# Attention transposes split into row halves over two pairs of PSUM banks, loads gated by GpSimd writes, and a longer count for one list's gathers

## The chip, the cores and the metric

The kernel runs on one core of one Trainium2 chip. The metric is the device time of one execution in microseconds (us), median of three runs. Engines are named as the profile names them: PE is the matrix engine, PEld its weight loads, DVE the vector engine, ACT the scalar engine, POOL is GpSimd, SP the engine that issues most transfers. "L416" is line 416 of the kernel.

## The reference

Windowed attention over 8 batches, 8 heads, 576 positions, head dimension 64, followed by a mixture of 8 experts with a fixed capacity. Cut to what is computed:

```
scores = q @ k^T / sqrt(D)                 # heads 0-3: 0 <= i-j < 32
                                           # heads 4-7: 0 <= i-j < 128 and (i-j) % 4 == 0
attn   = softmax(masked scores)
x      = (attn @ v) as [4608 tokens, 512]
logits = x @ w_gate                        # 8 experts
for idx in argsort(-logits.flatten()):     # best pair of token and expert first
    assign token to expert if the token is free and the expert holds < 576
out[tokens of e] = relu(x @ w1[e]) @ w2[e]
```

## The kernel before, in words

The program has two stages that follow each other. **Attention** works on 32 units, four for each batch: heads of kind 0 (plain window) or kind 1 (every fourth key), two units of two heads for each kind. A unit's 576 queries are nine blocks of 64 queries against 96 keys, two heads side by side in the 128 rows. It goes through the engines like this: PE makes the scores into two banks `pm` (L398); DVE masks them and keeps each row's extreme (L403) in `sc`; POOL subtracts that extreme (L409); PE transposes the nine blocks of `sc`, three into a bank of `pS` at a time (`turn`, L416); ACT takes the exponential out of `pS` into `et` (L412); PE multiplies with the values in two groups of five and four blocks into a bank of `px` (`values`, L424); ACT copies the sums (L428) and DVE divides (L433, L434) into `xs`. After the second unit of a kind, SP stores `xs` to the scratch tensor `xd`, and PE transposes `xs`, again three blocks into a bank, this time of `px` (`banks`, L475); ACT copies that to `xt`, from which the router's logits are made once per batch (L516, L548; L540 for the last). For each group of 128 tokens, DVE then makes 256 flags of "value reaches this step" (`coarse`, L647, into a ring of five tiles `pre`), and PE counts them per expert (L652) into a bank `pz` that keeps the sums until the end of the stage.

PSUM has eight banks: two `pm`, two `pS`, three `px`, one `pz`. The tiles for q, k and v are double-buffered by batch; a batch's twelve loads (eight of q and k, four of values) are issued on SP in a fixed order, each as soon as its tile is free of the batch two before.

**The experts' stage** makes eight lists of tokens one after the other, numbered r = 0 to 7 (the seventh list is r = 6). For a list it searches a threshold by counting (PE L660, DVE), turns the accepted tokens into row numbers (PE L1003, 18 small products, here called the placing), POOL gathers the rows of `xd` with five indirect transfers into `xg` (L1199), and PE transposes these by halves of 64 rows (`turn_halves`, L1254, 36 products). Then follow the two matrix products, `ph` (L1285) and `py` (L1327, L1330, L1332).

The order of instructions on each engine is fixed when the kernel is built. A planner (`Schedule`) takes operations with an engine, an estimated cost in ns, what they depend on and a `boost`; it computes a due time for each and places the earliest possible one by one. `lat` is an extra delay that it counts between an operation and its users; PSUM banks and their holders are part of the plan (`Pool`, `Buf`). The operation's `form` says in which shape of the array PE works; a change of form is counted at `T_TURN`. The chip runs every engine's list in that order, waiting on semaphores. The estimates set only the order.

Of the kernel before, what the change touches and what calls it, by code (L numbers as in the profile page):

```python
# [22 lines left out]
NE, FF = 8, 1024  # L23
# [19 lines left out]
ADDED, T_A, T_G = (("2", 0), ("1", 1), ("2", 1)), 2000, 4500  # L43
# [201 lines left out]
def attention(tc, ctx, C, load_const, T, xd, Lt, R):  # L245
# [24 lines left out]
    PM, PS, PV = Pool([banks_("pm", 2)]), Pool(banks_("pS", 2)), Pool(banks_("px", 3))  # L270
# [22 lines left out]
    ready = {}  # L293

    def load(b, kind, part):
# [5 lines left out]
        for t, src in ((QT, T["in_qd" if kind else "in_qp"]), (KT, T["in_kd" if kind else "in_kp"])):  # L301
            assert tuple(src.shape[1:]) == tuple(t[0][0].shape)
            ls.append(sp(1, lambda t=t, src=src: nc.sync.dma_start(t[kind][s][:, part], src[b][:, part]), load.old,
                            128 * 4 * S, b))
        ready["q", kind, b, part] = ls

    def load_values(b, kind):
# [4 lines left out]
        x = [sp(1, lambda c0=c0, c1=c1: nc.sync.dma_start(  # L312
            v[:, s, c0:c1], src[b].rearrange("p (c x) -> p c x", c=NV)[:, c0:c1]), before, 128 * (c1 - c0) * 4 * 65 * 4, b)
             for c0, c1 in ((0, 3), (3, NV))]
# [10 lines left out]
    class Unit:  # L325
# [17 lines left out]
        def build(self):  # L343
# [8 lines left out]
            for g, (c0, c1) in enumerate(GR):  # L352
# [6 lines left out]
                ex.append(e)  # L359
            olde = old("e", u % N_E)  # L360
            et = []
            for j in range(3):
                pt = Buf(PS)
                t = self.op("PE", 330, lambda j=j, pt=pt: self.turn(j, pt.tile, sc), [*ex[:1 + (j > 0)], ready["c", 1]], B_T, pt)
                uses.append(t)
                k = self.op("ACT", 400, lambda j=j, pt=pt: self.exps(j, pt.tile),
                            [t, *olde], B_T)
                pt.users.append(k)
                et.append(k)
# [44 lines left out]
        def turn(self, j, pt, sc):  # L414
            for x in range(3):
                nc.tensor.transpose(pt[:KB, 128 * x:128 * x + 128], sc[:, ORD[3 * j + x]], C["identf"])  # L416
# [39 lines left out]
    def banks(un, xs, done, usex):  # L456
# [8 lines left out]
        for i in range(3):  # L465
            pt = Buf(PV)

            def turn(i=i, pt=pt):
                t = pt.tile[:, :384]
                if kind:  # L470
                    t = t.rearrange("p (a c i) -> p a c i", a=2, c=3)
                else:
                    t = t.rearrange("p (a r c j) -> p a c r j", a=2, c=3, r=DIL)
                for c in range(3):
                    nc.tensor.transpose(t[:, :, c], xs[:, 3 * i + c].rearrange("p a d -> p (a d)"), C["identf"])  # L475
# [3 lines left out]
            def keep(i=i, pt=pt, f=nc.vector.tensor_copy if eng == "DVE" else act):  # L479
                t = pt.tile[:, :384].rearrange("p (a n) -> p a n", a=2)  # L480
                if kind:
                    f(xt[:, :, 192 * i:192 * i + 192], t)
                else:
                    x = xt.rearrange("p a (r n) -> p a r n", r=DIL)
                    f(x[:, :, :, 48 * i:48 * i + 48], t.rearrange("p a (r n) -> p a r n", r=DIL))

            t = un.op("PE", 330, turn, [*done, *oldt], late, pt)
            usex.append(t)
            k = un.op(eng, 450 + 100 * (eng == "DVE"), keep, [t, *oldt], late)
# [981 lines left out]
```

## Time and profile before

| | us |
|---|---|
| median of three runs | 653.42 (651.93 to 654.25) |
| profiled execution, its own time | 654.11 |
| span from first to last instruction | 652.3 |
| PE busy over the span | 615.5 (94%) |
| DVE busy | 451.9 (69%) |
| ACT busy | 305.8 (47%) |
| POOL busy | 196.8 (30%) |
| transfers | 100.18 MB, mean 154 GB/s |

Attention takes about the first quarter of the span, the experts the rest; between them lies a stretch in which the router works alone. A busy share is an average over stages with different limits, and PE's ends are modelled, so a price for a product is better read from the distance between two starts than from a duration. The profiled execution lies 0.7 us above the median.

### The profile page before, as it was taken

The page shows a single profiled execution, that of the slowest core. Times are in us where ns is not written, and L with a number is a line of the kernel's source. Part 1 is how long each engine was busy: PE and PEld are TensorE (multiplying, and loading weights), DVE is VectorE, ACT ScalarE, POOL GpSimd, SP SyncE. Part 2 cuts the span into 40 slices and gives each one's busy share as a digit, 9 for nine tenths or more (in the row PEclk, how much of TensorE's full clock was granted, in tenths as well). Part 3 has the DMA queues.
Part 4 walks back from the last instruction along what each step waited for, and adds up shares of the span by engine and source line. Part 5 has one row for each costly group of instructions (what it writes and reads, how often), then busy time and mean ns, then how long its engine had stood idle before and what let it go on. Part 6 is the DMA issues. An engine that isn't in the chain of part 4 may idle for free.

```text
span 652.3 us, 17966 instructions
## 1 busy us (share of the span) xinstructions
PE 615.5 (94%) x6748; PEld 530.0 (81%) x6749; DVE 451.9 (69%) x1930; ACT 305.8 (47%) x691; POOL 196.8 (30%) x326
## 2 busy tenths in 40 slices
PE   7999999997569999999999999999999989999994
PEld 5787888785449978977998898799889769989983
DVE  4668678885787888885997898699689746415200
ACT  3868788753038346844343433435244335325210
POOL 3434434330053156543016104301610530521011
PEclk9999999998579999999999999999999989999998
DMA  8998999823059378991164236207313734211010
GB/s 313 388 268 271 310 288 300 236 56 71 3 160 246 59 182 281 215 301 50 41 201 144 62 89 226 73 19 235 112 57 129 228 126 149 74 48 59 1 41 32
DMA packets 62680, 100.18 MB, mean 154 GB/s; under 512 B 7280, under 2 KB 26224, under 8 KB 62592
## 3 DMA queue, kind: packets, MB, share of 16 engines
q1 hardware_dynamic: 53216, 73.82, 35.6%
q0 software_dynamic: 9376, 25.21, 14.5%
q8 instruction: 53, 0.87, 0.5%
q14 instruction: 35, 0.29, 0.1%
HBM read 73.83 MB, written 18.87 MB: 142 GB/s over the span
## 4 chain that ended last, share of the span: by engine, by line
PE 70%; issue 12%; DVE 7%; DMA 4%; POOL 3%; ACT 2%; SPq 1%; POOLq 0%; DVEq 0%; ACTq 0%
PE ph L1285 25%; PE py L1327 18%; PE px L424 5%; PE pS L416 4%; PE pm L398 4%; PE pz L660 2%; PE px L475 2%; PE py L1330 2%; PE py L1332 2%; DVE sc L403 1%; POOL out L1353 1%; DMA xg<-xd,idx 1%; PE px L516 1%; DMA raw<-in_moe_w 1%; POOL xg L1199 1%
## 5 line engine op out<-in xcount | busy, mean ns | idle before, releaser
L1327 PE MATMUL py<-w2h,hb 128*128 128x512 f32 x512 | 165.9, 396 | 0.0
L1285 PE MATMUL ph<-xh,w1h 128*128 128x256 f32 (+1 forms) x512 | 138.6, 301 | 0.0
L1285 PE MATMUL ph<-xh,w1l 128*128 128x256 f32 (+1 forms) x512 | 136.3, 297 | 0.0
L1285 PE MATMUL ph<-xl,w1h 128*128 128x256 f32 (+1 forms) x512 | 135.9, 296 | 0.0
L1327 PEld LDWEIGHTS py<-w2h,hb 128*128 128x128 f32 x512 | 96.9, 189 | 20.0
L1071 ACT ACTIVATE hb<-ph 128x256 fp32r<-128x256 f32 (+2 forms) x192 | 59.9, 347 | 106.8 <-PE ph L1285 101.9
L1327 PE MATMUL py<-w2l,hb 128*128 128x512 f32 x256 | 100.4, 392 | 0.0
L1285 PEld LDWEIGHTS ph<-xh,w1h 128*128 128x128 f32 x512 | 91.4, 189 | 0.6 <-issue 0.3
L1285 PEld LDWEIGHTS ph<-xl,w1h 128*128 128x128 f32 x512 | 91.5, 189 | 0.1
L1285 PEld LDWEIGHTS ph<-xh,w1l 128*128 128x128 f32 x512 | 91.5, 190 | 0.0
L1353 POOL DMA_INDIRECT out<-y,tok x40 | 39.9, 998 | 148.6 <-ACT y L1071 68.7
L409 POOL TENSOR_TENSOR sc<-sc,mx 128x480 f32<-128x480 f32 x64 | 57.0, 912 | 90.2 <-DVE mx L403 90.2
L1071 ACT ACTIVATE y<-py 128x512 f32<-128x512 f32 (+1 forms) x40 | 23.9, 598 | 128.2 <-PE py L1327 97.9
L1305 DVE SCALAR_TENSOR_TENSOR hb<-ph,hb 128x320 fp32r<-128x320 f32 (+1 forms) x128 | 57.4, 453 | 32.6 <-ACT hb L1071 31.6
L403 DVE CUSTOM_DVE_ANT_0 sc<-pm,const 128x96 f32<-128x96 f32 x288 | 53.8, 253 | 21.8 <-PE pm L398 19.4
L1199 POOL DMA_INDIRECT xg<-xd,idx x40 | 43.6, 1089 | 64.7 <-issue 41.2
L1327 PEld LDWEIGHTS py<-w2l,hb 128*128 128x128 f32 x256 | 48.5, 189 | 9.3
L412 ACT ACTIVATE et<-pS 96x384 f32<-96x384 f32 x96 | 43.2, 484 | 23.8 <-PE pS L416 23.1
L1072 DVE TENSOR_TENSOR w2l<-raw,w2h 128x512 fp32r<-128x512 f32 x48 | 31.5, 684 | 20.2 <-ACT w2h L1071 19.9
L416 PE MATMUL pS<-const,sc 128*96 128x128 f32 x288 | 43.6, 279 | 1.0 <-ACT et L412 0.9
L1071 ACT ACTIVATE w1h<-raw 128x512 fp32r<-128x512 f32 x64 | 37.6, 628 | 6.2 <-DMA raw<-in_moe_w 6.1
L398 PE MATMUL pm<-k,q 64*64 64x96 f32 x1152 | 35.5, 253 | 2.7 <-DMA k<-in_kp 1.5
(188 smaller groups left out, 982.2 us busy)
## 6 DMA issues: line engine op xcount, KB each, us to landing
raw<-in_moe_w SPq DMA_DIRECT2D x128, 256.0 KB, 4.5
k<-in_kp SPq DMA_DIRECT2D x16, 304.0 KB, 6.0
k<-in_kd SPq DMA_DIRECT2D x16, 304.0 KB, 6.3
q<-in_qp SPq DMA_DIRECT2D x16, 288.0 KB, 5.4
q<-in_qd SPq DMA_DIRECT2D x16, 288.0 KB, 6.4
xd<-xs SPq DMA_DIRECT2D x64, 72.0 KB, 3.2
xd<-xs SPq DMA_DIRECT2D x16, 288.0 KB, 5.3
w2l<-raw POOLq DMA_DIRECT2D x16, 256.0 KB, 4.7
```

What stands on the lines that cost most here:

```text
L398: nc.tensor.matmul(o[w:w + 64], self.Q[c][r:r + 64], self.K[c][r:r + 64], start=True, stop=True)
L403: nc.vector.tensor_tensor_reduce(out=sc[:, c], in0=pms[g][:, c // 2 * KB:c // 2 * KB + KB], in1=mm[:, c if self.kind else min(1, c)], scal ...
L409: nc.gpsimd.tensor_tensor(sc[:, g::2], sc[:, g::2], mx[:, g::2, None].to_broadcast([128, n, KB]), op=OP.subtract)
L412: nc.scalar.activation(self.E0[:, 384 * j:384 * j + 384], pt[:KB, :384], AF.Exp, scale=-1.0)
L416: nc.tensor.transpose(pt[:KB, 128 * x:128 * x + 128], sc[:, ORD[3 * j + x]], C["identf"])
L424: nc.tensor.matmul(px[64 * a:64 * a + 64, x - c0], self.E0[:, w:w + 64], self.V[c][a], start=True, stop=True)
L1071: act = lambda o, i, f=AF.Copy: nc.scalar.activation(o, i, f)
L1199: nc.gpsimd.indirect_dma_start(out=xg[:n], out_offset=None, in_=xd, in_offset=bass.IndirectOffsetOnAxis(ap=box[0][:n, m:m + 1], axis=0))
L1285: nc.tensor.matmul(o, a[:, d * 128:d * 128 + 128], b[:, d, c0:c1], start=((d, i) == pairs[0]), stop=((d, i) == pairs[-1]))
L1305: hl = op("DVE", 335 if j == 0 else 400, lambda: nc.vector.scalar_tensor_tensor(hb[:, CAP + c0:CAP + c1], o, 0.0, hb[:, c0:c1], op0=OP.max ...
L1327: nc.tensor.matmul(py, x, w, start=(f + i == 0), stop=(f == NF - 1 and i == 2))
L1353: s = nc.gpsimd.indirect_dma_start(out=out, out_offset=bass.IndirectOffsetOnAxis(ap=box[1][:n, m:m + 1], axis=0), in_=y[:n], in_offset=None)
```

## The change

- `rows` (new) transposes a block as two halves of 64 rows, each into its own bank. `turn` and the transposes of `xs` use it, in groups of five and four blocks instead of three times three. `pS` becomes two tiles of two banks each and takes the transposes of `xs` too. ACT's exponential and copy take a group of five or four blocks out of two banks at once. `values` depends on its own group's exponential only.
- `px` shrinks from three banks to two, and the standing bank `pz` is gone from attention. The counts of flags go into a bank of `px`, for a whole batch in one operation (token group by token group for the last batch), and DVE adds them to a tile `cc` (`coarse_sum`). `pz` is made in the experts' stage, and cleared there by ACT.
- The loads of batch b+1 are planned during batch b. Ahead of each of the twelve, POOL writes one element of the tile to be loaded (`paced`), after one of batch b's eight subtractions; the load waits for that write.
- `T_GL`: the planner counts 7500 ns instead of 4500 after the gathers of list r = 6.

```diff
-ADDED, T_A, T_G = (("2", 0), ("1", 1), ("2", 1)), 2000, 4500
+ADDED, T_A, T_G, T_GL = (("2", 0), ("1", 1), ("2", 1)), 2000, 4500, 7500
...
-    PM, PS, PV = Pool([banks_("pm", 2)]), Pool(banks_("pS", 2)), Pool(banks_("px", 3))
+    PM, PV = Pool([banks_("pm", 2)]), Pool(banks_("px", 2))
+    PS = Pool([ps.tile([128, 2, 512], F32, name=f"pS{i}") for i in range(2)])
+
+    def rows(out, in_):
+
+        for h in range(2):
+            p = slice(64 * h, 64 * h + 64)
+            nc.tensor.transpose(out[:, h], in_[p], C["identf"][p, p])
...
+    def paced(after, to, deps):
+
+        un, e = after.pop(0)
+        return un.op("POOL", 100, lambda: nc.gpsimd.memset(to[:1, :1], 0.0), [e, *deps], B_A)
+
+    def load(b, kind, part, after=None):
...
+            deps = load.old
+            if after:
+                deps = [paced(after, to, deps)]
...
-            for j in range(3):
-                pt = Buf(PS)
-                t = self.op("PE", 330, lambda j=j, pt=pt: self.turn(j, pt.tile, sc), [*ex[:1 + (j > 0)], ready["c", 1]], B_T, pt)
+            for g, (c0, c1) in enumerate(GR):
+                n, pt = c1 - c0, Buf(PS)
+                t = self.op("PE", 62 * n, lambda c0=c0, c1=c1, pt=pt: self.turn(c0, c1, pt.tile, sc), [ex[g], ready["c", 1]],
+                            B_T, pt, "rows")
...
-                            [*(et[:2] if g == 0 else et), *ready["V", kind, b, g], *(y for y in oldx if y.eng == "PE")],
+                            [et[g], *ready["V", kind, b, g], *(y for y in oldx if y.eng == "PE")],
...
-        def exps(self, j, pt):
-            nc.scalar.activation(self.E0[:, 384 * j:384 * j + 384], pt[:KB, :384], AF.Exp, scale=-1.0)
+        def exps(self, c0, c1, pt):
+            n = c1 - c0
+            e = self.E0[:, 128 * c0:128 * c1].rearrange("p (x h q) -> p h x q", x=n, h=2)
+            nc.scalar.activation(e, pt[:KB, :, :64 * n].rearrange("p h (x q) -> p h x q", x=n), AF.Exp, scale=-1.0)
...
     def coarse(c0, c1, x, late):
+        gs, pt, last = [], Buf(PV), c1 == NCH
         for c in range(c0, c1):
             g, used, use_ = PRE.take()
             f = op("DVE", 290, lambda c=c, g=g: R.coarse(c, g), [x, *used], late)
-            counted[0] = op("PE", 60, lambda c=c, g=g: R.coarse_counts(c, g), [f, ready["c", 3], counted[0]], late,
-                            form="whole")
+            gs.append((c, g, f, use_))
+        k = None
+        for part in [[y] for y in gs] if last else [gs]:
...
+        pt.users.append(op("DVE", 200, lambda: R.coarse_sum(pt.tile), [k], late))
...
     for u in range(4 * B):
         b = u // 4
-        if u % 4 == 0 and b:
+        Unit(u).build()
+        if u % 4 == 3 and b + 1 < B:
+            after = [steps[8 * b + 8 * i // 12] for i in range(12)]
             for kind in range(2):
-                load(b, kind, 0)
-                load_values(b, kind)
-                load(b, kind, 1)
-        Unit(u).build()
+                load(b + 1, kind, 0, after)
+                load_values(b + 1, kind, after)
+                load(b + 1, kind, 1, after)
...
-                   lat=2500 if r <= DENSE else T_G, dma=T_GM if 0 < r <= DENSE else 0)
+                   lat=2500 if r <= DENSE else T_GL if r == NE - 2 else T_G, dma=T_GM if 0 < r <= DENSE else 0)
```

The planner gives every engine another order. Three places show it. On PE, in attention, the transposes of one unit (`sc` to `pS`), its products with the values (`v`, `vo`), and transposes of a kind's result (`xs`); first before, then now:

```order
63 L416 MATMUL pS_136<-const_61,sc_110 96x128 x3
64 L416 MATMUL pS_137<-const_61,sc_110 96x128 x3
65 L424 MATMUL px_138<-v_104,et 64x65 x10
66 L424 MATMUL px_139<-vo_106,et 64x65 x8
67 L416 MATMUL pS_136<-const_61,sc_110 96x128 x3
68 L416 MATMUL pS_137<-const_61,sc_108 96x128 x3
69 L424 MATMUL px_140<-v_105,et 64x65 x10
```

```order
195 L277 MATMUL pS_136<-const_61,sc_108 96x64 x10
196 L277 MATMUL pS_137<-const_61,sc_108 96x64 x8
197 L445 MATMUL px_134<-v_103,et 64x65 x10
198 L445 MATMUL px_135<-vo_105,et 64x65 x8
199 L277 MATMUL pS_136<-const_61,xs_116 128x4x16 x10
200 L277 MATMUL pS_137<-const_61,xs_116 128x4x16 x8
```

Three products of 128 columns became ten or eight of 64, and `xs` goes to `pS`. Over the whole stage 432 transposes in 53 unbroken runs became 864 halves in 60 runs, and PE changes its form 158 times instead of 137.

On DVE, late in attention, the flags (`pre`) around the choice of experts for one batch (`Lt`, `M`, `key`); first before, then now:

```order
669 L647 TENSOR_SCALAR pre_129<-const_63,V_73 128x256
670 L647 TENSOR_SCALAR pre_130<-const_63,V_73 128x256
671 L647 TENSOR_SCALAR pre_126<-const_63,V_73 128x256
672 L647 TENSOR_SCALAR pre_127<-const_63,V_73 128x256
673 L566 COPY Lt<-px_140 128x40
674 L763 TENSOR_REDUCE M<-Lt 128x5
675 L765 TENSOR_SCALAR key_75<-M 128x5
```

```order
690 L826 TENSOR_REDUCE bits<-bt 128x5
691 L680 TENSOR_SCALAR pre_128<-const_63,V_73 128x256
692 L680 TENSOR_SCALAR pre_124<-const_63,V_73 128x256
693 L680 TENSOR_SCALAR pre_125<-const_63,V_73 128x256
694 L680 TENSOR_SCALAR pre_126<-const_63,V_73 128x256
695 L690 TENSOR_TENSOR cc<-cc,px_134 128x16
696 L690 TENSOR_TENSOR cc<-cc,px_135 128x16
697 L422 ISA sc_108,mx_112<-pm_132,const_60 128x96
```

Before, 12 of the 36 flag operations stood ahead of the 24th unit's masking, 15 between the 26th's and the 29th's, and 9 behind the last. Now 5 stand in the first half of the stage, none from there to the middle of the 29th unit's masking, 22 between there and the 31st's, and 9 behind the last. The sums into `cc` are new.

On PE, the placing for list r = 6 (`ptx<-rx,ob`, the first of its 18 products); first before, then now:

```order
3962 L1327 MATMUL py_3040<-w2h_3066,hb_3101 128x512
3963 L1327 MATMUL py_3040<-w2l_3082,hb_3101 128x512
3964 L1327 MATMUL py_3040<-w2h_3066,hb_3101 128x512
3965 L1003 LDWEIGHTS ob
3966 L1003 MATMUL ptx_3041<-rx,ob 128x40
```

```order
3900 L1323 MATMUL ph_3513<-xh,w1h_3538 128x320
3901 L1323 MATMUL ph_3513<-xh,w1l_3554 128x320
3902 L1323 MATMUL ph_3513<-xl,w1h_3538 128x320
3903 L1040 LDWEIGHTS ob
3904 L1040 MATMUL ptx_3516<-rx,ob 128x40
```

It stood behind the ninth `py` product of the list before and now stands ahead of the last nine `ph` products; the transposes of the gathered rows stand behind the 57th `py` product both times.

## Rows read from the trace of the kernel before

**Rows 1.** Busy time of each engine by stretch, with PE clock and transfers.

```profile
core 0: us, PE busy (x) PEld busy (x) DVE busy (x) ACT busy (x) POOL busy (x), PEclk, DMA share, GB/s
0.00:158.40 158.40, 149.46 (x3131) 120.70 (x3132) 112.02 (x795) 110.47 (x253) 57.57 (x72) 1.00 0.83 255
22.00:112.00 90.00, 87.56 (x1889) 71.88 (x1885) 66.67 (x483) 71.12 (x162) 35.62 (x40) 1.00 0.95 297
112.00:135.00 23.00, 22.16 (x470) 18.71 (x468) 19.58 (x124) 16.76 (x38) 7.13 (x8) 1.00 0.76 213
525.77:529.41 3.64, 3.64 (x10) 2.83 (x9) 3.62 (x9) 0.00 (x0) 1.07 (x2) 0.53 0.29 114
```

**Rows 2.** Groups by line, to 235 us: count | busy us, mean ns | idle before.

```profile
L416 PE MATMUL pS<-const,sc 128*96 128x128 f32 x288 | 43.6, 279 | 1.0 <-ACT et L412 0.9
L475 PE MATMUL px<-const,xs 128*128 128x128 f32 x144 | 22.2, 280 | 1.9 <-DVE xs L434 1.3 <-DVE xt L482 0.3
L412 ACT ACTIVATE et<-pS 96x384 f32<-96x384 f32 x96 | 43.2, 484 | 23.8 <-PE pS L416 23.1
L566 DVE COPY Lt<-px 128x32 f32<-128x32 f32 (+1 forms) x8 | 1.5, 192 | 7.1 <-PE px L548 4.9 <-PE px L540 2.2
```

**Rows 3.** PE in order of time: start us, duration us, line, product.

```profile
72.64 0.87 PE L475 MATMUL px<-const,xs 128*128 128x128 f32 x6
73.34 0.82 PE L416 MATMUL pS<-const,sc 128*96 128x128 f32 x6
74.09 0.80 PE L424 MATMUL px<-v,et 96*64 96x65 f32 x20
```

**Rows 4.** PE in order of time, the gathered rows' transposes by halves.

```profile
350.81 1.20 PE L1254 MATMUL ph<-const,xg 64*128 64x64 f32 x32
351.85 0.41 PE L1254 MATMUL ptx<-const,xg 64*128 64x64 f32 x4
352.19 0.50 PE L1327 MATMUL py<-w2h,hb 128*128 128x512 f32 x1
```

**Rows 5.** DVE in order of time, runs of flags late in attention.

```profile
123.46 1.75 DVE L647 TENSOR_SCALAR pre<-const,V 128x256 bf16<-128x256 bf16 x5 [0.33 <-PE pz L652]
131.92 1.06 DVE L647 TENSOR_SCALAR pre<-const,V 128x256 bf16<-128x256 bf16 x5
```

**Rows 6.** One group of `px`, in order of time, PE's write to DVE's read.

```profile
66.38 0.80 PE L424 MATMUL px<-v,et 96*64 96x65 f32 x20
68.24 0.49 DVE L434 TENSOR_TENSOR xs<-px,rec 128x320 f32<-128x320 f32 x1 [0.28 <-DMA k<-in_kd]
```

**Rows 7.** Transfers of the first 160 us: share by 4 us; queue, packets, MB, share.

```profile
DMA  5999999979999599989998999989999670333506
...
q1 hardware_dynamic: 34770, 40.25, 81.5%
```

**Rows 8.** POOL in order of time: one small write.

```profile
517.88 0.09 POOL L1352 MEMSET spacer<- 1x1 f32 x1
```

**Rows 9.** PE in order of time, end of attention.

```profile
158.37 1.24 PE L540 MATMUL px<-wgp,xt 128*32 128x8 f32 x76 [0.37 <-ACT xt L271]
```

**Rows 10.** PE in order of time, placing and transposes of list r = 6.

```profile
505.85 0.31 PE L1285 MATMUL ph<-xl,w1h 128*128 128x320 f32 x1
505.99 0.39 PE L1327 MATMUL py<-w2h,hb 128*128 128x512 f32 x1
...
508.06 0.62 PE L1003 MATMUL ptx<-rx,ob 128*128 128x40 bf16 x18
...
519.68 0.95 PE L1254 MATMUL ph<-const,xg 64*128 64x64 f32 x24
521.18 0.46 PE L1254 MATMUL ph<-const,xg 64*128 64x64 f32 x8 [0.54 <-DMA xg<-xd,idx]
524.35 0.46 PE L1254 MATMUL ptx<-const,xg 64*128 64x64 f32 x4 [2.71 <-DMA xg<-xd,idx]
```

**Rows 11.** Gathers of list r = 6, time from issue to landing.

```profile
DMA to landing us min/median/max: 3.7/4.1/7.3
```

More of the change, by code (lines that the diff above doesn't have):

```diff
@@ L291, in const @@
         ready["c", i] = sp(1 if i < 3 else 2, lambda: load_const(i), (), 128 * 1500, 0)
-    ready = {}
-    def load(b, kind, part):
+    ready, steps = {}, []
+    def paced(after, to, deps):
+        un, e = after.pop(0)
+        return un.op("POOL", 100, lambda: nc.gpsimd.memset(to[:1, :1], 0.0), [e, *deps], B_A)
+    def load(b, kind, part, after=None):
         s = b % 2
@@ L311, in load_values @@
         before = old("v", kind, s)
-        x = [sp(1, lambda c0=c0, c1=c1: nc.sync.dma_start(
-            v[:, s, c0:c1], src[b].rearrange("p (c x) -> p c x", c=NV)[:, c0:c1]), before, 128 * (c1 - c0) * 4 * 65 * 4, b)
-             for c0, c1 in ((0, 3), (3, NV))]
+        x = []
+        for c0, c1 in ((0, 3), (3, NV)):
+            deps = [paced(after, v[:, s, c0], before)] if after else before
+            x.append(sp(1, lambda c0=c0, c1=c1: nc.sync.dma_start(
+                v[:, s, c0:c1], src[b].rearrange("p (c x) -> p c x", c=NV)[:, c0:c1]), deps, 128 * (c1 - c0) * 4 * 65 * 4, b))
         ready["V", kind, b, 0] = x
@@ L409, in shift, with turn @@
             nc.gpsimd.tensor_tensor(sc[:, g::2], sc[:, g::2], mx[:, g::2, None].to_broadcast([128, n, KB]), op=OP.subtract)
-        def exps(self, j, pt):
-            nc.scalar.activation(self.E0[:, 384 * j:384 * j + 384], pt[:KB, :384], AF.Exp, scale=-1.0)
-        def turn(self, j, pt, sc):
-            for x in range(3):
-                nc.tensor.transpose(pt[:KB, 128 * x:128 * x + 128], sc[:, ORD[3 * j + x]], C["identf"])
+        def exps(self, c0, c1, pt):
+            n = c1 - c0
+            e = self.E0[:, 128 * c0:128 * c1].rearrange("p (x h q) -> p h x q", x=n, h=2)
+            nc.scalar.activation(e, pt[:KB, :, :64 * n].rearrange("p h (x q) -> p h x q", x=n), AF.Exp, scale=-1.0)
+        def turn(self, c0, c1, pt, sc):
+            for x in range(c0, c1):
+                rows(pt[:KB, :, 64 * (x - c0):64 * (x - c0) + 64], sc[:, ORD[x]])
         def values(self, c0, c1, px):
@@ L499, in coarse, with count @@
             f = op("DVE", 290, lambda c=c, g=g: R.coarse(c, g), [x, *used], late)
-            counted[0] = op("PE", 60, lambda c=c, g=g: R.coarse_counts(c, g), [f, ready["c", 3], counted[0]], late,
-                            form="whole")
-            use_.append(counted[0])
+            gs.append((c, g, f, use_))
+        k = None
+        for part in [[y] for y in gs] if last else [gs]:
+            def count(part=part):
+                for c, g, *_ in part:
+                    R.coarse_counts(c, g, pt.tile, c == c0, c == c1 - 1)
+            k = op("PE", 10 + 50 * len(part), count, [*(y[2] for y in part), ready["c", 3], k], late,
+                   buf=None if k else pt, form="whole")
+            for y in part:
+                y[3].append(k)
+        pt.users.append(op("DVE", 200, lambda: R.coarse_sum(pt.tile), [k], late))
     lt_ = {}
@@ L584, in idle @@
                 keep_clock(nc, warm, fill, int(max(0, gap - 400) / 430))
-    op("DVE", 300, lambda: nc.vector.memset(R.pz[:, :256], 0.0), (), B_P)
     load(0, 0, 0)
@@ L639, in __init__, with work @@
         nc.gpsimd.memset(self.PR, 0.0)
-    def work(self, ctx):
+        nc.gpsimd.memset(self.cc, 0.0)
+    def work(self, ctx, ps):
+        self.pz = ps.tile([128, 512], F32, name="pz")
         self.pw = ctx.enter_context(self.tc.tile_pool(name="r_work", bufs=2))
@@ L1044, in moe @@
     pw = ctx.enter_context(tc.tile_pool(name="m_w", bufs=1))
-    R.work(ctx)
+    R.work(ctx, ps)
     ctx.enter_context(tc.manual_schedule())
```

63 lines of the change are left out of this document (33 added, 30 removed).

## Prediction

> **What bounds the kernel now.** I read the busy times by stretch first. Attention ends at 158.4 us with the last products of the router [rows 9], and up to there PE is busy 149.5 us of 158.4, in 22 to 112 us 87.6 of 90; DVE 112.0, ACT 110.5, POOL 57.6, and PE's clock is at its full level throughout [rows 1]. So attention is a stage in which PE works nearly without a gap and the other engines have a third or more to spare. The reader is to see two more things in the same rows. Transfers are at 95% in 22 to 112 us, and fall only after that: their share over the first 160 us is 81.5%, or 130 us of full work [rows 1, 7]. And in 112 to 135 us DVE is at 19.6 of 23, 85%: the second limit lies close there. The groups by line then show what PE spends its time on: the transposes of scores (288) and of results (144) have no idle time ahead of them worth naming, 1.0 and 1.9 us [rows 2]; nobody holds them up, they simply are PE work. In the experts' stage PE has one gap that this change speaks of, at the seventh list: 0.54 and 2.71 us of waiting for gathered rows, and behind it nine `py` products at a granted clock of 0.53, after a PE that had stood still for most of 3 us [rows 10, 1].
>
> The sum is made against the profiled execution: 654.1 us, of which 652.3 are its span. That is 0.7 above the median of the runs, within their spread of 2.3.
>
> **Transposes.** Before: twelve whole blocks in one run took from 72.64 to 74.09, 1.45 us, and the first six of them 0.70 [rows 3]. That is 0.117 a block, 0.121 with the run's end. By halves the trace shows them at the gathered rows: 32 halves in 351.85 - 350.81 = 1.04 us, 0.0325 each; with the last four, 36 halves took 352.19 - 350.81 = 1.38, so 18 blocks cost 0.077 each with the run's end, and the end of a run alone 1.38 - 36 x 0.0325 = 0.21 [rows 4]. There the stationary operand has 128 columns, here 96 or 128; both stream 64 columns from 64 rows into two banks in turn, so I take the price over.
> - Upper end, by price per block: 432 x (0.121 - 0.077) = 19.0 us.
> - Lower end, with every run paying its end: before 432 x 0.117 + 53 x 0.05 (1.45 - 12 x 0.117) = 53.2; now 864 x 0.0325 + 60 x 0.21 = 40.7; a gain of 12.5.
>
> The runs here hold 14 halves on average, the measured one 36, so neither end fits; I take the middle, 15.7 us. The 21 added changes of form I take as covered by these ends. [...]
>
> **What of it reaches the stage's end.** Three parts of the stage can't give their share.
> - The late pile on DVE. In 112 to 135 us DVE did 19.6 us of work, 15 flag operations among it. The order now puts 22 between the 29th and the 31st unit's masking, seven more, at 0.21 to 0.35 each (five in 1.06 or in 1.75 us [rows 5]), and five or six sums into `cc`; no row shows a sum, the nearest is the copy of logits from PSUM, 0.19 us [rows 2]. That makes 19.6 + 7 x 0.28 + 6 x 0.19 = 22.7 of DVE work where there was 23 of time. DVE becomes what this stretch waits for, and it keeps its length. Its share of the gain, 15.7 x 23/158 = 2.3 us, goes.
> - The start. The first units wait for their first loads; the first batch's share, 2 us, I count at half: 1.0.
> - The two `px` banks. A group holds its bank from PE's first product to the end of DVE's division, 66.38 to 68.73, 2.35 us [rows 6]. Two groups per unit on two banks make 2.35 us per unit as a floor, and the logits and counts of a batch use the same two. POOL's 40 subtractions, two per unit, say that a unit takes 90 / 20 = 4.5 us now [rows 1], and it would take 4.5 - 15.7 / 32 = 4.0. It fits, at six tenths of the banks' time and more with the logits, so some products will wait; I take off 1.0, and keep 0 and 8 as ends (0.25 us for each of 32 units).
>
> Left: 15.7 - 2.3 - 1.0 - 1.0 = 11.4 us. The last result's transposes and copies come in two groups instead of three, which shortens the end; against that stands one sum into `cc` on the way from the last count to the router's search, 0.2 us and its two hand-overs. I set both against each other.
>
> **What is hidden.** Twelve writes for seven batches on POOL, 84 x 0.09 = 7.6 us [rows 8], on an engine that is busy 57.6 of 158.4. Behind each on POOL's list stands a unit's subtraction, and PE's transposes wait for that; if the cover went, three writes per unit would put 0.3 us on it, at most 8 us over 28 units. ACT's exponentials are the same columns in 64 instead of 96 instructions; by columns alone they cost the 43 us that they cost now [rows 2], so a loss needs two-bank reads to be dearer, which no row shows, and ACT has 48 us to spare. The clearing of `pz` lies on ACT while DVE chooses.
>
> **Seventh list.** The placing moves ahead by nine `py` products, 0.229 each (48 in 519.68 - 508.06 less 0.6 for the placing and two small ones), and nine of `ph` at 0.14: 2.06 + 1.26 = 3.3 us. The transposes stay behind the 57th `py`. The last gather landed at about 524.3, at the latest end of 3.7 to 7.3 us [rows 10, 11]; 3.3 us earlier is 521.0, and the last transposes are due at 519.7 + 1.0 = 520.7. So 3.25 us of waiting shrink to 0.3. With the gap goes the slow clock: nine products took 3.64 instead of 9 x 0.229 = 2.06 [rows 1], 1.6 us. Together 4.5. Between 0, if the gathers land no earlier because the weights' loads hold them, and 4.9. DVE's search steps move ahead too; if the placing then waits for DVE, that wait would stand on PE instead, up to the same 3 us. I take 4.3.
>
> Sum: 654.1 - 11.4 - 4.3 = 638.4. The tail's sign and the rounding left aside, I forecast 638 us.
>
> **Rivals.**
> - *All of it arrives.* PE stays the bound, `px` and DVE keep up because the planner's order interleaves them: 654.1 - 19.0 - 4.9 = 630. For it: DVE has 46 us to spare over the stage. Against it: where the flags now stand.
> - *The banks or DVE take over.* Products with the values wait for `px`, or DVE's queue holds the divisions back: 8 us of the 11.4 go, 654.1 - 3.4 - 4.3 = 646. For it: 2.35 us of holding and 85% on DVE. Against it: before, 112.0 of 158.4 on DVE on the whole.
> - *Halves don't run beside each other.* Then 864 halves cost what 432 blocks cost, PE is as busy as before, plus run ends: 654.1 - 4.3 + 2 = 652. Rows 4 speak against it. [...]
> - *Starved by its own gates (slower).* Before, transfers ran far ahead: 95% busy until 112 us, quiet at the end [rows 1, 7]. Now a load is let go only in the batch before, and SP keeps its order, so one late release holds the stores and loads behind it. The stage needs 130 us of transfers; at full rate that leaves little air in 147. If each of the seven gated batches makes PE wait 3 us, that is 21 us, and a PE that stands still falls to half clock as at the seventh list: 654.1 - 11.4 - 4.3 + 21 + some 3 = 662. It is slower than before from 2.3 us of waiting per batch on (15.7/7). Against it: a load's release lies three to four units, some 15 us, ahead of its use.
>
> **How the numbers follow.** My forecast 0.52, all of it 0.17, banks or DVE 0.20, no overlap 0.04, starved 0.07. The measurement tells 0.3%, about 2 us, from no change. Forecast, all and banks are faster; no overlap falls half and half on faster and same; starved is slower in two thirds, the rest between. That gives 0.91 faster, 0.03 same, 0.06 slower. The range for 8 in 10 reaches from the full gain to the case of the banks with a little more lost: 629 to 648.
>
> **What would show it.** In the profile after: attention's last L572 near 147 us (146 to 149); a run of 18 halves within 0.6 to 0.8 us; PE busy above 92% up to there; between the 29th and 31st unit DVE at 95% or more with PE gaps put down to DVE flags; no gap of over 0.5 us and no slow clock at the seventh list. It would be wrong if PE shows gaps put down to loads of q, k or v after the first 20 us, if the products with the values wait for `px` in most units, or if a run of 18 halves takes 1.2 us or more.

## The result, and the profile after

The changed kernel takes 662.36 us (median of 6 runs, 655.04 to 664.43) against 653.84 us before (6 runs): a ratio of 1.0121, 95% interval 1.0091 to 1.0152. It is slower by 8.5 us. The forecast was 638, with 629 to 648 as range. The profiled execution took 664.43 us, its span 662.7. Here and below the ratios leave out the runs that lie over 1.5% above the fastest of their kernel, and they need not be the quotient of the two medians.

The first view is the busy time by stretch of the changed kernel; its columns are those of [rows 1].

```profile
0.00:170.20 170.20, 144.00 (x3637) 117.77 (x3637) 109.43 (x801) 106.24 (x206) 60.78 (x157) 0.90 0.80 240
22.00:112.00 90.00, 79.03 (x2036) 65.74 (x2038) 60.76 (x461) 63.26 (x122) 36.73 (x97) 0.92 0.91 272
...
45.00:48.40 3.40, 3.27 (x60) 2.77 (x56) 2.08 (x11) 2.87 (x4) 1.33 (x5) 0.51 0.94 275
...
137.00:144.00 7.00, 5.43 (x114) 4.75 (x118) 6.84 (x40) 4.74 (x8) 1.99 (x2) 0.75 0.13 24
144.00:150.00 6.00, 6.00 (x116) 5.35 (x110) 3.63 (x25) 1.54 (x4) 1.82 (x2) 0.50 0.01 3
...
525.00:545.00 20.00, 20.00 (x119) 16.47 (x118) 7.85 (x21) 4.14 (x8) 9.69 (x23) 1.00 0.69 223
```

In 22 to 112 us PE was busy 87.6 of 90 before [rows 1] and is busy 79.0 now, at a mean granted clock of 0.92 instead of 1.00; in 45.0 to 48.4 and in 144 to 150 us it was 0.51 and 0.50, which is called half clock below. That PE is less busy isn't less work done sooner, for attention ends later: its last router products start at 169.64 and are done at 170.1, where before they were done at 159.6 [rows 9]. So attention is 10.5 us longer; from there to the end of the span it is 492.5 us now and 492.7 before. The last line is the seventh list: PE busy 20.00 of 20, at full clock, where [rows 1] had 0.53 behind a gap.

The second view is PE in order of time (start, duration, line, product, then in brackets the idle time ahead and what ended it), the gaps of over 0.5 us that the trace puts down to "issue", one run of 18 halves with the row behind it, and three rows that come up later.

```profile
42.73 0.41 PE L417 MATMUL pm<-k,q 64*64 64x96 f32 x9 [1.73 <-issue]
...
71.41 0.71 PE L277 MATMUL pS<-const,sc 64*96 64x64 f32 x18
72.05 0.69 PE L445 MATMUL px<-vo,et 96*64 96x65 f32 x16
...
74.83 0.45 PE L445 MATMUL px<-v,et 96*64 96x65 f32 x8 [1.74 <-issue]
...
92.08 0.39 PE L445 MATMUL px<-v,et 96*64 96x65 f32 x6 [2.20 <-issue]
...
100.31 0.32 PE L277 MATMUL pS<-const,sc 64*96 64x64 f32 x5 [0.60 <-issue]
...
120.72 0.56 PE L417 MATMUL pm<-k,q 64*64 64x96 f32 x15 [2.04 <-issue]
...
131.27 0.20 PE L684 MATMUL px<-oh,pre 128*128 128x8 bf16 x2 [1.29 <-issue]
...
140.65 0.77 PE L277 MATMUL pS<-const,sc 64*96 64x64 f32 x10 [1.22 <-POOL sc L428]
...
143.04 1.87 PE L417 MATMUL pm<-k,q 64*64 64x96 f32 x36
...
169.64 0.50 PE L572 MATMUL px<-wgp,xt 128*32 128x8 f32 x21 [1.16 <-issue]
...
298.63 0.66 PE L697 MATMUL pz<-G,ohr 128*128 128x64 bf16 x9 [3.17 <-ACT ohr L832]
```

The run of 18 halves takes 72.05 - 71.41 = 0.64 us: that price was right. The gaps are what is new. They stand in the middle of runs (9 of 36 scores left, 8 of 20 products with the values left), and the brackets name no semaphore, bank or load that they wait for.

Where they stand can be counted. I numbered all of PE's recorded instructions in order of time, from 0: weight loads, products, and the 144 entries of PE's sequencer, nearly all of them waits. The gaps at 42.73, 74.83, 92.08, 100.31, 120.72, 131.27 and 169.64 stand at numbers 1729, 3265, 4033, 4289, 5313, 5825 and 7361. The differences are 1536, 768, 256, 1024, 512 and 1536: each a multiple of 256. Here and below a gap at such a boundary is counted from the start of one instruction to the start of the next: 1.97 us at 42.73, of which 1.73 are PE's idle time. The transfers have a queue that the page calls "instruction". From the page of the changed kernel (queue, packets, MB, share of 16 engines):

```profile
q8 instruction: 56, 0.92, 0.6%
```

Every packet on it has 16,384 bytes, 56 of them for PE's 14,510 recorded instructions, one per 259. In the page of before it reads:

```profile
q8 instruction: 53, 0.87, 0.5%
```

That is 53 for 13,607, one per 257. Call the 256 instructions from one boundary to the next a block, and a packet of this queue a fetch. Laid beside PE's order in the changed kernel, one fetch starts in each of the 20 blocks between 20 and 135 us, 1.3 to 6.0 us after PE has entered the block, and takes 1.1 us on average; at each of the gaps above PE goes on 1.3 to 1.6 us after one has landed. From these numbers I read that PE's instructions come by these packets, one block ahead, and that PE stands when one is late; the page counts the packets to the same 16 engines as the loads (0.6% and 35.4% of their span for q8 and q1). That reading is the theory "instruction fetch" of the experiments. Between 20 and 135 us the boundary gaps of over 0.3 us add up to 12.1 us.

### The profile page after: what moved, and what is told of

Its sections match the earlier page's. It is cut to its first block, busy times and chain, and to the rows that moved or that the text cites. A ratio compares the mean times of both kernels' runs of the same rounds, so it can differ in the third digit from the quotient of the medians.

```text
span 662.7 us, 18928 instructions
## 1 busy us (share of the span) xinstructions
PE 609.7 (92%) x7183; PEld 526.7 (79%) x7183; DVE 448.5 (68%) x1936; ACT 301.5 (45%) x645; POOL 200.0 (30%) x411
## 3 DMA queue, kind: packets, MB, share of 16 engines
q1 hardware_dynamic: 53216, 73.82, 35.4%
## 4 chain that ended last, share of the span: by engine, by line
PE 56%; issue 11%; DVE 5%; POOL 2%; DMA 2%; ACT 1%; SPq 1%; POOLq 0%; DVEq 0%
PE ph L1323 25%; PE py L1365 19%; PE pz L697 2%; PE py L1368 2%; PE py L1370 2%; DMA raw<-in_moe_w 1%; POOL out L1391 1%; PE px L445 1%; PE ph L1292 1%; PE pz L776 1%; PE pS L277 1%; SPq L1127 1%; DVE G L711 1%; DMA xg<-xd,idx 1%; PE pm L417 1%
## 5 line engine op out<-in xcount | busy, mean ns | idle before, releaser
L428 POOL TENSOR_TENSOR sc<-sc,mx 128x480 f32<-128x480 f32 (+1 forms) x64 | 57.6, 914 | 92.2 <-DVE mx L422 64.2
L433 ACT ACTIVATE et<-pS 96x640 f32<-96x640 f32 (+1 forms) x64 | 39.5, 643 | 22.2 <-PE pS L277 21.9
L417 PE MATMUL pm<-k,q 64*64 64x96 f32 x1152 | 38.9, 268 | 5.1 <-issue 3.8
L1109 ACT ACTIVATE w1h<-raw 128x512 fp32r<-128x512 f32 x64 | 37.8, 628 | 10.1 <-DMA raw<-in_moe_w 10.0
L417 PEld LDWEIGHTS pm<-k,q 64*64 64x64 f32 x1152 | 31.4, 146 | 9.9 <-issue 5.1
```

The lines of the kernel that those rows point to most:

```text
L417: nc.tensor.matmul(o[w:w + 64], self.Q[c][r:r + 64], self.K[c][r:r + 64], start=True, stop=True)
L428: nc.gpsimd.tensor_tensor(sc[:, g::2], sc[:, g::2], mx[:, g::2, None].to_broadcast([128, n, KB]), op=OP.subtract)
L433: nc.scalar.activation(e, pt[:KB, :, :64 * n].rearrange("p h (x q) -> p h x q", x=n), AF.Exp, scale=-1.0)
L1109: act = lambda o, i, f=AF.Copy: nc.scalar.activation(o, i, f)
```

## The experiments

The theories: *instruction fetch*; *gates* (GpSimd's writes, or loads let go late: the prediction's slower rival); *px banks*; *flags* (the late pile on DVE). Each median stands beside that of before in the same session. Differences to the changed kernel go across sessions, against its first median of 662.36 us; its second was 662.11, with single runs from 654 to 666, so 3 or 4 us are less sure than the ratios to before.

**Loads without pacing.** In the main loop of the changed kernel:

```
-        Unit(u).build()
-        if u % 4 == 3 and b + 1 < B:
-            after = [steps[8 * b + 8 * i // 12] for i in range(12)]
+        if u % 4 == 0 and b:
...
+        Unit(u).build()
```

> The changed kernel with the loads of q, k and v put where the kernel before had them, without the 84 writes of GpSimd; halves, bank pairs and seventh list stay. Theory 'instruction fetch': PE's instructions come in blocks of 256 by the DMA engines, and by halves PE is through a block before the next has landed while transfers run at 90% and more. PE has as many instructions here and transfers are as dense, so gaps of 1 to 2.5 us that the trace puts down to nothing (issue) stay, at least three before 140 us, each 256 PE instructions or a multiple apart, half-clock stretches behind them, and the time is 655 to 664. Theory 'gates' (writes in GpSimd's order hold up the subtractions behind them, PE waits): the gaps go, attention's last router product ends at 146 to 152 us and the time is 640 to 648.

Measured: 658.63 us, before 654.77, ratio 1.0068 (1.0036 to 1.0101). The trace has 14.2 us of gaps at block boundaries between 20 and 135 us (12.1 in the changed kernel), the last router products end at 165.7. The gates aren't the cause of the gaps. The 3.7 us under the changed kernel aren't shown to be the writes' price: without them the planner also gives DVE another order (13 flag operations instead of 22 between the middle of the 29th and the 31st unit's masking), and from the last subtraction to the last router product it takes 13.8 us instead of 17.5.

**Fewer instructions, more work.** The scores' blocks transposed whole:

```
-                rows(pt[:KB, :, 64 * (x - c0):64 * (x - c0) + 64], sc[:, ORD[x]])
+                f = pt.rearrange("p a n -> p (a n)")
+                nc.tensor.transpose(f[:KB, 128 * (x - c0):128 * (x - c0) + 128], sc[:, ORD[x]], C["identf"])
...
```

> The changed kernel with the scores' 288 blocks transposed whole again, four in the first bank of a pair and the fifth in the second; the results' 144 stay in halves; order on all engines, banks and GpSimd's writes as in the changed kernel. 'Instruction fetch': 576 PE instructions fewer of some 6,700 in attention, so a block of 256 lasts longer and most gaps go (none to two of over 1 us before 140 us); the work on PE rises by 288 x (0.117 - 0.077) = 11.5 us against the halves, but the half clock goes with the gaps: 646 to 655, faster than the changed kernel though PE has more to do. 'Gates' and 'px banks' (two banks hold up the products with the values): nothing that they speak of changes and PE has 11 us more: 662 to 672.

Measured: 654.51 us, before 654.77, ratio 0.9975 (0.9942 to 1.0009). The boundary gaps between 20 and 135 us fall from 12.1 to 2.5 us; two of over 1 us are left before 140 us, at 19.64 and 98.16. It is 7.9 us faster than the changed kernel, with 576 instructions fewer and more work in the others: what counted was the number.

**Fewer transfers, same instructions.** In the changed kernel's loads, and the same in those of the values:

```
+            m = 128 if b < 2 else 1
-            ls.append(sp(1, lambda to=to, src=src: nc.sync.dma_start(to, src[b][:, part]), deps, 128 * 4 * S, b))
+            ls.append(sp(1, lambda to=to, src=src: nc.sync.dma_start(to[:m], src[b][:m, part]), deps, 128 * 4 * S, b))
```

> The changed kernel whose loads of q, k and v for the batches 2 to 7 bring one row of 128 each: the work goes on with the data of the batches 0 and 1, so most of what is loaded is left out, and the results are of other data. Order on all engines, GpSimd's writes and each load's issue stay. 'Instruction fetch': the fetches start within 1 us of their block's change instead of 2 to 6, no gap of over 0.5 us put down to nothing between 45 and 140 us, clock at full level there, attention's last router product at 143 to 150 us, time 636 to 645. 'Gates' in the sense of writes that stand in GpSimd's way, and 'px banks': these stay as they are, so attention ends beyond 160 us and the time is over 655.

And the control, the same edit in the kernel before:

> Control to the run with few loads: the kernel before, whose loads of q, k and v for the batches 2 to 7 bring one row of 128 each (most of what is loaded is left out; results are of older data). If the gain of few loads comes by the fetches, it belongs to the changed kernel with its 256 instructions in under 5 us; before needs some 6 us for 256, has one gap of over 1 us, and gains 1 to 3 us: 650 to 653, attention's end at 156 to 159 us. If transfers slow PE or the other engines in some other way, before gains as the changed kernel did, 10 us or more: under 645.

Measured: the changed kernel with few loads 648.07 us, 14.3 less than with all, ratio to before 0.987 (0.9792 to 0.9949); before with few loads 652.92, 1.7 less than its session's 654.59, ratio 0.997 (0.9946 to 0.9994). By stretch, the changed kernel with few loads:

```profile
22.00:112.00 90.00, 83.17 (x2336) 69.89 (x2338) 68.47 (x527) 71.70 (x142) 42.43 (x114) 1.00 0.48 91
45.00:128.00 83.00, 76.65 (x2154) 64.29 (x2150) 68.23 (x508) 67.58 (x131) 38.60 (x98) 1.00 0.44 78
```

And before with few loads:

```profile
22.00:112.00 90.00, 88.43 (x1896) 72.83 (x1895) 67.73 (x495) 72.34 (x165) 36.35 (x41) 1.00 0.44 87
```

In 90 us the changed kernel does 2336 products with few loads and 2036 with all. Before does 1896 and 1889 [rows 1]: it loses almost nothing to the loads. Between 45 and 128 us no boundary gap is left and the granted clock is 1.00. Counted by blocks between 20 and 135 us:

| kernel | us for 256 PE instructions | from entering the block before to the fetch's start: mean (longest) | boundary gaps over 0.3 us, start to start, sum |
|---|---|---|---|
| before | 6.10 | 2.5 (4.5) | 2.2 |
| changed | 5.55 | 2.8 (6.0) | 12.1 |
| changed, few loads | 4.98 | 1.2 (3.9) | 3.2, all before 29 us |
| before, few loads | 5.98 | 0.6 (2.0) | 0 |
| scores whole | 5.64 | 2.5 (4.7) | 2.5 |

Under dense loads, by an estimate from these rows, the changed kernel is served a block in 2.8 + 1.1 + 1.4 = 5.3 us on average (start of the fetch, the packet, going on), and a single one took 8.2 (from 92.08 to 100.31). The same sum is 5.0 for before, which needs 6.10 us for 256 instructions and is served in time but for 2.2 us of boundary gaps; by halves PE needs 4.98 with few loads, so by this estimate the fetch sets the pace. My expectation was nearly met in this stretch (fetches start after 1.2 us, not within 1) and missed at the end: half clock from 128.7 to 138.9 stayed (the mean granted clock up to 158.5 us is 0.94), attention ended at 158.4, not by 150, and the time is above the 636 to 645 expected. That is the next cause.

**Flags earlier.** In the changed kernel's list of boosts, one number:

```
-... = 4500, 8000, 4000, -5200, 4000, -105500, 650, 650, 300, 800
+... = 4500, 8000, 4000, -5200, 4000, -80000, 650, 650, 300, 800
```

> The changed kernel with one number of the planner altered (the flags' boost -80000 instead of -105500): 17 of the 22 flag operations that stood between the 29th and the 31st unit's masking now stand between the 23rd and the 27th. The changed kernel's end of attention, from the subtraction of the 29th unit (139.52) to the last router product (170.16), is 30.6 us, 6.5 longer than before's 24.1. Theory 'flags': DVE's flags between the halves of a masking keep scores from PE, PE waits and falls to half clock; with them gone this stretch takes 24 to 27 us, the clock stays full until some 14 us before the end, the stretch ahead, bound by fetches, stays as it is: 656 to 660. Theory 'px banks': counts and products with the values share two banks, which is the same here: the stretch stays at 29 us or more, 661 to 665.

Measured: 655.57 us, before 654.01, ratio 1.0001 (0.9962 to 1.0039); 6.8 less than the changed kernel; in the profiles attention ends at 165.3 instead of 170.1. One thing in my expectation was misread: 139.52 is the first subtraction of the 30th unit, not of the 29th. From the last subtraction to the last router product it is 17.5 us in the changed kernel (152.7 to 170.1), 14.0 here, 12.2 before. The same two stretches as above, here:

```profile
137.00:144.00 7.00, 6.91 (x196) 5.42 (x186) 5.69 (x39) 5.78 (x13) 2.48 (x3) 1.00 0.74 165
144.00:150.00 6.00, 5.97 (x170) 5.19 (x167) 5.05 (x40) 3.92 (x9) 2.52 (x3) 1.00 0.30 54
```

In the changed kernel PE does 230 products in these 13 us, here 366: DVE at 6.84 of 7 comes late with its maskings, GpSimd's subtraction behind it too, PE waits 1.22 us for that up to 140.65 and is at a granted clock of 0.50 from 140.5 to 150.8. DVE in order of time in the changed kernel shows four flags and two sums ahead of the masking that this wait hangs on (from 138.38), and five flags between its halves:

```profile
137.31 0.87 DVE L680 TENSOR_SCALAR pre<-const,V 128x256 bf16<-128x256 bf16 x4
138.09 0.37 DVE L690 TENSOR_TENSOR cc<-cc,px 128x16 f32<-128x16 f32 x2
138.38 0.25 DVE L422 CUSTOM_DVE_ANT_0 sc<-pm,const 128x96 f32<-128x96 f32 x1
...
139.09 0.25 DVE L422 CUSTOM_DVE_ANT_0 sc<-pm,const 128x96 f32<-128x96 f32 x1
139.27 0.08 DVE L422 DVE_READ_ACCUMULATOR2_ANT mx<- 128x1 f32 x1
139.27 1.80 DVE L680 TENSOR_SCALAR pre<-const,V 128x256 bf16<-128x256 bf16 x5
```

**Both causes away.** Few loads and flags early:

> Both suspects away: the changed kernel with one row of 128 per load of q, k and v for the batches 2 to 7 (most of what is loaded is left out; results are of older data) and with the flags' boost at -80000. If fetch and flags are the two causes and add up: no gap at a boundary of 256 instructions between 45 and 130 us, subtraction of the 29th unit at 127 to 130 us, end of attention 24 to 26 us behind it at 151 to 155 us, 640 to 645 us in all. If one cause hides the other, 646 to 650 as with few loads alone.

Measured: 645.29 us, ratio 0.9834 (0.9768 to 0.99); attention ends at 152.6. They add in part: the flags are worth 2.8 us here, 6.8 where instructions come late.

**Pacing alone.** In the kernel before, with `paced` and its memsets as in the changed kernel:

```
-        if u % 4 == 0 and b:
...
         Unit(u).build()
+        if u % 4 == 3 and b + 1 < B:
+            after = [steps[8 * b + 8 * i // 12] for i in range(12)]
...
```

> The kernel before with the 84 writes of GpSimd and loads let go by them; whole blocks, three px banks, seventh list as before. 'Instruction fetch': PE has its old number of instructions and needs some 6 us for 256 of them; pacing adds no gap at these boundaries: 652 to 656. 'Gates': GpSimd's writes stand ahead of subtractions and PE waits for these by 3 us per batch: 660 to 670. In between, 656 to 659, pacing would have a price of its own beside the fetches, as the changed kernel without it (3.8 us faster) suggests.

Measured: 657.75 us, before 654.01, ratio 1.0052 (1.0023 to 1.008). The in-between case: 3.7 us. Its profiled execution was one of the quicker ones (655.3); attention ends in it at 160.0 us, 0.4 later than before, and it shows no wait that I could put the 3.7 us down to. How pacing costs them, by the writes or by the order that the planner then finds, stays open.

**Two px banks alone** (in the kernel before):

```
-    PM, PS, PV = Pool([banks_("pm", 2)]), Pool(banks_("pS", 2)), Pool(banks_("px", 3))
+    PM, PS, PV = Pool([banks_("pm", 2)]), Pool(banks_("pS", 2)), Pool(banks_("px", 2))
...
```

The bank that the filling products at the start hold is now the second instead of the third.

> The kernel before with two px banks instead of three, the eighth bank left unused; everything else as before, in the order that the planner then finds. Priced as in the prediction (1.0 us, at most a few of the 32 units wait): 653 to 657. Theory 'px banks' (two banks are what stretches attention): gaps of PE put down to DVE's division in many units, 660 to 670.

Measured: 661.55 us, before 654.01, ratio 1.0113 (1.0054 to 1.0171). My 1.0 us is 7.5. From the last subtraction to the last router product it takes 17.7 us instead of 12.2; PE in order of time there:

```profile
162.03 0.87 PE L475 MATMUL px<-const,xs 128*128 128x128 f32 x3 [0.25 <-DVE xs L434]
163.55 0.90 PE L475 MATMUL px<-const,xs 128*128 128x128 f32 x3 [0.65 <-DVE xt L482]
165.11 0.90 PE L475 MATMUL px<-const,xs 128*128 128x128 f32 x3 [0.65 <-DVE xt L482]
165.94 0.28 PE L540 MATMUL px<-wgp,xt 128*32 128x8 f32 x4
166.59 1.24 PE L540 MATMUL px<-wgp,xt 128*32 128x8 f32 x76 [0.37 <-ACT xt L271]
```

Here groups of the results' transposes wait for a copy out of `px` (0.65 us twice), at half clock from 162.0 us: a group of three takes 0.87 to 0.90 us there and 0.49 to 0.55 between 150.4 and 154.2. Boundary gaps are 3.7 us in this profile, 2.2 before, so a part of the 7.5 may be theirs. In the changed kernel the results' transposes have the bank pairs, so the 7.5 can't be carried over whole; its own share wasn't measured apart.

**Seventh list.** Alone, in the kernel before, with `T_GL` at 7500:

```
...
-                   lat=2500 if r <= DENSE else T_G, dma=T_GM if 0 < r <= DENSE else 0)
+                   lat=2500 if r <= DENSE else T_GL if r == NE - 2 else T_G, dma=T_GM if 0 < r <= DENSE else 0)
```

> The kernel before with the seventh list's gathers counted at 7500 and nothing else. Theory 'it arrives': the gap of 3.25 us at the seventh list and the slow nine products behind it go, 4 us in all: 648 to 651. Theory 'given back elsewhere in the experts' stage': 652 to 655, with a new gap at another list.

And taken out of the changed kernel:

```
-ADDED, T_A, T_G, T_GL = (("2", 0), ("1", 1), ("2", 1)), 2000, 4500, 7500
+ADDED, T_A, T_G, T_GL = (("2", 0), ("1", 1), ("2", 1)), 2000, 4500, 4500
```

> The changed kernel with the seventh list's gathers counted at 4500 as before; attention as changed. If the seventh list's gain arrives in the changed kernel too and the gap near 297 us has another cause: the gap at the seventh list is back (3 us and slow products behind it), the gap near 297 stays within 1 to 3.5 us, 666 to 668. If the longer count causes the gap near 297: that gap falls to about 1 us with full clock, and the time stays at 661 to 664.

Measured: alone 649.51 us, before 654.77, ratio 0.991 (0.9877 to 0.9944); taken out 668.29, before 654.56, ratio 1.0183 (1.0098 to 1.0267). It gives 5.3 us in the one and 5.9 in the other (6.2 against the changed kernel's own median of that session, 662.11). The gap returns where it is taken out:

```profile
537.58 0.68 PE L1292 MATMUL ptx<-const,xg 64*128 64x64 f32 x4 [2.06 <-DMA xg<-xd,idx]
```

**The changed kernel once more,** with no edit.

> The changed kernel once more, for a second profile. 'Instruction fetch': gaps put down to nothing stand again at multiples of 256 PE instructions, though at other places among these than in the first profile, since each depends on how loads fall; their sum before 140 us 9 to 15 us. The gap near 297 us: between 1 and 3.5 us, and where it is under 2 us no half clock behind it. Time 660 to 664.

Measured: 662.11 us, before 654.56, ratio 1.0081 (1.0033 to 1.0129). PE in order of time:

```profile
76.19 0.45 PE L445 MATMUL px<-v,et 96*64 96x65 f32 x8 [1.67 <-issue]
...
92.97 0.39 PE L445 MATMUL px<-v,et 96*64 96x65 f32 x6 [0.31 <-issue]
...
118.69 0.56 PE L417 MATMUL pm<-k,q 64*64 64x96 f32 x15 [0.71 <-issue]
...
129.53 0.20 PE L684 MATMUL px<-oh,pre 128*128 128x8 bf16 x2 [1.57 <-issue]
...
297.15 0.66 PE L697 MATMUL pz<-G,ohr 128*128 128x64 bf16 x9 [3.00 <-ACT ohr L832]
```

The same instructions (8, 6, 15 and 2 left of their runs), other lengths, and no gap of over 0.3 us at the boundary near 42.73: 10.1 us of boundary gaps between 20 and 135 us. Of 17 gaps of over 1 us there, in three profiles of the changed kernel (this one, the first, and the one with the old count) and one of before, all 17 stand on a boundary of 256, to within the one or two records that some profiles lack. The gap near 297 us is there again, with 6.8 us of half clock behind it as in the first profile (granted 0.50 in 298 to 304 us there, 0.91 as the mean of 280 to 320 us in both). Before it was 1.02 us, in these rows of PE in order of time, of which the first is its only boundary gap of over 1 us, shown as 0.85 since a weight load came a little ahead:

```profile
29.87 0.62 PE L424 MATMUL px<-v,et 96*64 96x65 f32 x13 [0.85 <-issue]
...
285.74 0.46 PE L660 MATMUL pz<-G,ohr 128*128 128x64 bf16 x9 [1.02 <-ACT ohr L795]
```

In the chain of waits of the first profile (start, length, what) it hangs on ACT, and ACT on a load of weights that took 8.88 us to land:

```profile
287.44 8.88 DMA raw<-in_moe_w
296.34 0.58 ACT w1h L1109
...
297.43 1.16 ACT ohr L832
298.63 0.66 PE pz L697 x9
```

In the chain of before the load that it hangs on took 5.88 us:

```profile
278.09 5.88 DMA raw<-in_moe_w
284.00 0.46 ACT w1h L1071
```

The longer count isn't its cause: without it the gap is 3.14 us and followed by half clock too, for 3.4 us at 298.2 (mean of 280 to 320 us: 0.96). Why that load takes longer to land than before wasn't settled.

**Towards a better version.** Scores whole and flags early, by the two edits above; the same with the last six units by halves; and the first of the two without pacing, by the edit of the first experiment. The second adds, in `turn` (and its match in `exps`):

```
+U_H = 26
...
+                if self.u >= U_H:
+                    rows(pt[:KB, :, 64 * (x - c0):64 * (x - c0) + 64], sc[:, ORD[x]])
+                    continue
```

> The changed kernel with the scores' blocks whole and the flags' boost at -80000: both causes taken away by other means than leaving out loads. By the two runs apart (7.9 and 6.8 us under the changed kernel's 662.4) the sum would be 647.7 if they add, 654 if one hides the other. Expected 647 to 652; the stretch from the last subtraction to the last router product takes 14 us instead of 17.

> As the kernel with whole scores and early flags, but the scores of the last six of the 32 units by halves, where transfers are no longer dense. 'Instruction fetch': no new gap at a boundary behind 120 us, and 54 blocks at 0.04 us, 2 us, are saved at most: 645 to 652, at or up to 2 us under its sister. If halves cost for another reason (two-bank reads, changes of form), it is slower than its sister by 1 us or more.

> A version made from what the runs point to: scores' blocks whole, results' by halves, flags' boost at -80000, seventh list at 7500, and the loads where the kernel before had them, without GpSimd's 84 writes. By the sister with the writes (650.6) and the run without them (3.8 us faster than the changed kernel), 645 to 649, under the 649.5 of the seventh list alone. If the writes' price shows only where instructions arrive late, it is 649 to 652, as the sister.

Measured: 650.62 (ratio 0.9946, 0.9913 to 0.9979), 651.94 (0.9974, 0.9945 to 1.0004) and 650.35 us (0.9943, 0.9911 to 0.9975). All beat the changed kernel, none the kernel before with the seventh list alone at 649.51. The kernel with late halves is 1.3 us slower than its sister, with intervals that overlap, so my sign for another cost of halves (slower by 1 us or more) is neither confirmed nor ruled out. Taking the pacing out gives 0.3 us here, against 3.7 for adding it to the kernel before.

## Why the prediction was wrong

- **What bounds the kernel: the step that failed.** I wrote that nobody holds up the transposes, "they simply are PE work", and that PE works nearly without a gap. So I priced 432 added products and 432 added weight loads by PE's time alone. The term that is missing is the supply of instructions: 864 more, used up in 4.98 us per 256 with few loads, where before took 5.98, while transfers stand at 95% [rows 1]. With few loads the changed kernel gains 14.3 us and before 1.7, so 12.6 of difference, more than the whole forecast of 11.4 and about half of the 24 us between 638 and 662. No rival had it.
- **The price of halves.** Right: 18 in 0.64 us, forecast 0.6 to 0.8. With few loads 256 instructions take 4.98 us instead of 5.98.
- **The late pile on DVE.** Seen, in the right place: DVE at 98% in 137 to 144 us, forecast 95%. Mis-sized: I let the stretch keep its length and counted 2.3 us of lost gain. Moving the flags gains 6.8 us where instructions come late and 2.8 with few loads; PE, after its wait of 1.22 us up to 140.65, ran at a granted clock of 0.50 up to 150.8.
- **Two px banks.** 1.0 was taken of 0 to 8; alone, in the old form, it is 7.5. A floor for a whole unit says nothing of the end of attention, where results, logits and values meet.
- **GpSimd's writes.** Priced at nothing, with 8 us as the most. Adding the pacing to the kernel before costs 3.7 us; removing it gives 3.7 where DVE's order changed with it, and 0.3 in the kernel with whole scores and early flags. What the price is of isn't shown.
- **Seventh list.** Forecast 4.3, measured 5.3 and 5.9; the gap and the slow products went as said.
- **After attention.** 492.5 against 492.7 us, though the seventh list gained: the wait near 297 us is 2.2 us longer and 6.8 us behind it are at a granted clock of 0.50. Not foreseen, not settled.
- **The rival at 662.** "Starved by its own gates" had the number and not the cause: between 20 and 160 us no gap of PE is put down to a load, and without gates the gaps stay. None of the three signs that I named as proof of error came up; two of the signs named for the forecast failed (last L572 at 169.64 instead of near 147 us, PE busy 84.6% up to there instead of above 92%). The error was in the supply of instructions, of which no row that I had read tells.
- **Small readings.** 158.4 us is where the last router products start, not where attention ends (159.6). And by the prediction's own rule for the rivals the shares of same and slower are nearer to 0.04 and 0.05 than to 0.03 and 0.06.

With fetch and flags out of the way the changed kernel takes 645.3 us, 8.7 under before. Before gains 1.7 by few loads too, so 7.0 is the fairer figure, and the seventh list has 5.3 to 5.9 of it. That leaves, as an estimate across sessions, 1 to 2 us of the forecast's 11.4 for halves, banks and writes together. So the fetch isn't the whole of the miss: the pacing, the two banks and the wait near 297 us are in the rest, and their shares weren't measured apart.

## What to carry to other kernels

Before an edit that splits PE's work into more and smaller instructions, count PE's instructions per microsecond (weight loads too) and look at the transfers' share in the same stretch: here the kernel before, with 256 in 6.10 us and transfers at 95%, had 2.2 us of boundary gaps between 20 and 135 us, and the changed kernel, with 256 in 4.98 when few loads run, had 12.1 with transfers at 91%. A gap "issue" in the middle of a run is worth numbering PE's instructions for. And in a stage where PE is the bound, halves of an edit are best timed one by one: here one number for a late list gave all that there was.

## What the runs showed of the hardware

- The instruction queue q8 had 56 packets of 16,384 bytes for 14,510 recorded PE instructions in the changed kernel, one per 259, and 53 for 13,607 before, one per 257. In the changed kernel a packet took 0.9 to 2.2 us once it had started; between 20 and 135 us, with transfers at 91% in 22 to 112 us, it started 1.3 to 6.0 us after PE had entered a block of 256 instructions, and with transfers at 44% in before's control 0.6 us after on average.
- PE went on 1.3 to 1.6 us after a packet had landed, at each of the seven gaps of the first profile.
- All 17 gaps of over 1 us between 20 and 135 us, in three profiles of the changed kernel and one of before, stood on a boundary of 256 instructions as numbered above, to within one or two records. Their lengths differ: idle 2.20, 3.30 and 0.31 us at the sixth last product near 92 us in three profiles of the changed kernel; 1.73, 0.35 and no gap of over 0.3 us at the boundary near 42.
- In the changed kernel, from 144 to 150 us, PE was busy 6.00 of 6.00 us and stayed at a granted clock of 0.50, until 150.8 us.
